# A softmax-attention and gated-MLP kernel: sign words of the weights by GpSimd, shift and sign in one VectorE instruction, weight pieces in pairs, the second k load with its channels reordered

## The chip, the cores and the metric

The kernel runs on one core of a Trainium2 chip. The metric is the device time of one execution in microseconds (us), the median of three runs. Five engines take part: TensorE (PE in the profile, its weight loads PEld), VectorE (DVE), ScalarE (ACT), GpSimd (POOL) and SyncE (SP), which only issues DMAs here.

## The reference

Attention without a score matrix: softmax of q over the head's channels, softmax of k over the sequence, their product with v, and on the result a gated MLP in which a learned matrix mixes positions.

```
q_s = softmax(q, axis=-1); k_s = softmax(k, axis=2)          # q, k, v: (8, 8, 576, 64)
kv  = einsum('bhsd,bhse->bhde', k_s, v)
x   = einsum('bhsd,bhde->bhse', q_s, kv)  -> (8, 576, 512)
h   = gelu_tanh(x @ w_in)                                    # w_in: (512, 1024)
u, v = h[..., :512], h[..., 512:]
v_n = (v - mean(v)) / sqrt(var(v) + 1e-6) * g_ln
v_s = einsum('ts,bsd->btd', w_sg, v_n) + b_sg                # w_sg: (576, 576)
out = x + (u * v_s) @ w_out                                  # w_out: (512, 512)
```

w_in, w_out and w_sg of the gated MLP come to the kernel as inputs; w_in and w_out are float64 in its memory, everything else float32.

## The kernel before

**Precision.** A product of two float32 matrices is made of three matmuls in the type fp32r: each operand is split into a high part (a cast) and a low part (the difference), and high x high, high x low and low x high are summed in PSUM. So each operand costs, beside the matmuls, one cast (mostly ACT) and one subtraction (DVE or POOL).

**Steps and order.** The work of the eight batches is cut into named steps such as `hu_mm 3 1`. The string PLAN (lines 33 to 137) writes all of them in one order. The class InOrder (line 144) makes every engine issue its instructions in exactly that order, so PLAN fixes five queues at once, SP's DMAs among them; an instruction that waits holds up everything behind it on its engine. A letter after a step (V, A or G) puts it on VectorE, ScalarE or GpSimd. All instructions but the matmuls (line 241) are recorded at line 154.

**Steps for one batch.** load_q, load_k, load_kt and load_v bring the operands. q is shifted by its maximum (q_max, q_swapm, q_top, q_sub), exponentiated, summed, scaled (q_inv, q_mul) and transposed (q_turn). For k, kt_max takes the maximum of each channel from the transposed load; kt_put and kt_get send the maxima through memory so that every partition holds all of them (kmt); k_sub (line 403) subtracts them and k_exp takes the exponential. kv_mm and x_mm are the attention products; x_high and x_low split x. hv_mm makes the v half of the MLP (hv_stat, hv_pow, hv_norm, hv_high, hv_low are the LayerNorm and its split: vnh, vnl), hu_mm the u half (hu_gelu), sg_mm the mixing of positions, gate the product with u, gate_high and gate_low its split (gh, ulow), out_mm the last product, out_add and out_rest the sum with x, out_store the store. The last block of the last batch is done in two halves: last_mm, last_add, last_store.

**The start.** Batch 0 has its own steps (q0_..., k0_..., x0_..., hu0_mm), which transpose on TensorE with an identity matrix (eye) that is loaded (load_eye). The weights arrive meanwhile, as float64: two 32-bit words to a number, the top one with sign and exponent. converter (line 274) makes a float32 of them in five steps for each piece of 128 columns (w_in: wi_..., eight pieces; w_out: wo_..., four pieces): a: ACT scales the top word, taken as a float, by 2^-112; b: DVE shifts the result left by three; c: DVE takes the sign bit of the top word with an AND and joins it with an OR; d: DVE shifts the low word right by 29 and joins it; h: ACT casts to the high part; l: POOL, DVE, or TensorE and ACT (wi_x and `wi_l A`) make the low part. c and d are scalar_tensor_tensor instructions, with two tensors as inputs (STT below), b is a tensor_scalar with one. The raw words lie in tiles that are later reused (raw_vnl holds pieces 2 and 3 of w_in, raw_vnh 0 and 1, raw_wo_h and raw_wo_l 4 to 7; raw_x_h and raw_x_l those of w_out); the words under work lie in four slots of the output (ot_i, ot_o). w_sg is split by ws_h and ws_l, 640 columns at a time. hu0_mm needs pieces 0 to 3, hv_mm needs 4 to 7.

## Time and profile before

| what | value |
|---|---|
| median of 3 runs | 504.43 us (503.58 to 504.43) |
| profiled execution | 504.85 us, its span 503.1 us |
| granted TensorE clock | 1.00 |
| instructions | 9377 |
| DMA | 57.28 MB, mean 114 GB/s |

How to read it: the span is the part of the execution that the profile covers; the time on top of it, 1.75 us here, is outside every engine's records. Busy time of an engine is a sum over its instructions; neighbouring instructions overlap a little, so the step from one start to the next can be shorter than a duration. A row of groups gives line, engine, operation, tiles, shape and count, then busy time and the mean in ns of one, then the idle time of the engine just before them with its releaser.

### The profile page before, as it was taken

To read this page: it belongs to the slowest core of one execution; us is meant where nothing else is said; L and a number is where in the kernel's file an instruction comes from. 1 tells how busy PE (TensorE), PEld (TensorE's weight loads), DVE (VectorE), ACT (ScalarE), POOL (GpSimd) and SP (SyncE) were. 2 spreads that over 40 slices of the span, in tenths; PEclk is the share of its full clock that TensorE was granted. 3 is DMA by queue.
4 is the path that set the end of the run, shared out by engine and by line. 5 is a ranking of instruction groups with operands and counts; after the bars stand their busy time and mean duration, and the time that the engine had idled before them with its cause. 6 is when DMAs were issued, how large, how long until landed. Compare 5 with 4: busy or idle time off the path is not lost.

```text
span 503.1 us, 9377 instructions
## 1 busy us (share of the span) xinstructions
PE 484.9 (96%) x3834; PEld 444.4 (88%) x3834; DVE 347.9 (69%) x563; ACT 246.9 (49%) x434; POOL 171.6 (34%) x180
## 2 busy tenths in 40 slices
...
GB/s 309 327 407 225 151 196 26 77 171 137 145 42 71 170 172 128 33 191 124 122 72 71 182 140 26 143 26 213 163 1 1 61 36 1 1 48 1 25 7 112
DMA packets 20495, 57.28 MB, mean 114 GB/s; under 512 B 3042, under 2 KB 3428, under 8 KB 20452
## 3 DMA queue, kind: packets, MB, share of 16 engines
...
q14 instruction: 13, 0.11, 0.1%
...
## 4 chain that ended last, share of the span: by engine, by line
PE 82%; DVE 5%; DMA 4%; ACT 3%; issue 3%; POOL 2%; SPq 1%; POOLq 0%; DVEq 0%; ACTq 0%
PE ps L241 82%; DVE qq L154 2%; DMA kk<-kt 1%; DMA kmt<-scr 1%; DMA eye<-identity 1%; POOL kk L154 1%; SPq L154 1%; POOL qe L154 1%; POOL ulow L154 1%; DVE kk L154 0%; DVE ulow L154 0%; DVE u L154 0%; DVE ot_i L154 0%; DVE wo_l L154 0%; ACT qs L154 0%
## 5 line engine op out<-in xcount | busy, mean ns | idle before, releaser
L154 POOL TENSOR_TENSOR rs<-ve,half 128x1 f32<-128x1 f32 x36 | 27.4, 765 | 111.8 <-DVE ve L154 101.8
L241 PE MATMUL ps<-ulow,wo_h 128*128 128x288 f32 x256 | 55.7, 296 | 1.2 <-DVE ulow L154 1.2
L241 PE MATMUL ps<-gh,wo_h 128*128 128x288 f32 x256 | 56.0, 298 | 0.5 <-DVE o L154 0.5
L241 PE MATMUL ps<-ws_h,vnl 128*128 128x288 f32 x256 | 54.9, 296 | 1.0 <-DVE vnl L154 1.0
L241 PE MATMUL ps<-gh,wo_l 128*128 128x288 f32 x256 | 55.5, 295 | 0.0
L241 PE MATMUL ps<-ws_h,vnh 128*128 128x288 f32 x256 | 55.2, 297 | 0.1
L154 DVE TENSOR_TENSOR u<-ps,u 128x576 f32<-128x576 f32 x32 | 23.9, 753 | 44.9 <-PE ps L241 44.7
L241 PE MATMUL ps<-ws_l,vnh 128*128 128x288 f32 x256 | 54.9, 296 | 0.0
L154 ACT CAST gh<-u 128x576 fp32r<-128x576 f32 x32 | 21.4, 672 | 64.9 <-DVE u L154 64.9
L154 ACT ACTIVATE u<-ps 128x576 f32<-128x576 f32 (+2 forms) x36 | 21.4, 603 | 53.9 <-PE ps L241 53.8
L241 PEld LDWEIGHTS ps<-ws_h,vnh 128*128 128x128 f32 x256 | 41.7, 188 | 1.9 <-ACT u L154 1.2
L241 PEld LDWEIGHTS ps<-gh,wo_h 128*128 128x128 f32 x256 | 41.7, 188 | 1.9 <-DVE o L154 0.8
L241 PE MATMUL ps<-x_h,wi_h 128*128 128x288 f32 (+2 forms) x256 | 42.4, 300 | 0.9 <-ACT u L154 0.9
L154 ACT ACT_TABLE_LOAD x30 | 38.5, 1283 | 9.3 <-PE ps L241 5.3
L241 PEld LDWEIGHTS ps<-ulow,wo_h 128*128 128x128 f32 x256 | 41.2, 188 | 1.7 <-DVE ulow L154 1.7
L241 PEld LDWEIGHTS ps<-ws_h,vnl 128*128 128x128 f32 x256 | 41.3, 188 | 1.2 <-DVE vnl L154 1.2
L154 POOL TENSOR_TENSOR ulow<-u,gh 128x576 fp32r<-128x576 f32 x12 | 17.3, 1439 | 73.5 <-DVE ulow L154 50.2
L241 PEld LDWEIGHTS ps<-x_h,wi_h 128*128 128x128 f32 x256 | 36.5, 188 | 5.8 <-ACT u L154 2.8
L241 PE MATMUL ps<-x_l,wi_h 128*128 128x288 f32 (+2 forms) x256 | 41.5, 297 | 0.1
L241 PEld LDWEIGHTS ps<-gh,wo_l 128*128 128x128 f32 x256 | 41.4, 188 | 0.0
L241 PEld LDWEIGHTS ps<-ws_l,vnh 128*128 128x128 f32 x256 | 41.3, 188 | 0.0
L241 PE MATMUL ps<-x_h,wi_l 128*128 128x288 f32 (+2 forms) x256 | 41.3, 296 | 0.0
...
## 6 DMA issues: line engine op xcount, KB each, us to landing
...
```

Source lines behind the costliest of these rows:

```text
L154: ins = op(*args, **kw)
L241: tc.keep_in_program_order(nc.tensor.matmul(*args, **kw))
```

## The change

Five things change.

1. **The sign.** A new step b on GpSimd multiplies the top words, taken as floats, by 0.0 in place; what is left of each is its sign. Step c on VectorE then shifts t and joins the sign in one STT, so a piece takes two VectorE instructions instead of three. Step a may go to GpSimd (`wi_a 2 G`, 1, 0, and `wo_a` 2, 0).
2. **Pairs.** Pieces 4+5 and 6+7 of w_in and 0+1 and 2+3 of w_out (PAIRED) are handled together in instructions of 1024 columns. The words under work lie in one tile (o) that is the output tile later. w_sg is split two pieces at a time, 1280 columns.
3. **k.** For batches 2 to 7 the transposed load has its rows in another order, so that the 256 maxima that k_sub reads lie side by side; before, it read every fourth word.
4. **The end.** `last_mm 7 0, last_mm 7 1` stand ahead of `last_add 7 0`; before, `last_add 7 0` stood between them.
5. **The order.** PLAN is written anew, for all engines. load_eye is the seventh DMA instead of the tenth. Of the twelve k_subs, GpSimd had eight and VectorE four; now GpSimd has four and VectorE eight.

The diff of the functions that the prediction speaks of (PLAN left out but for lines that show steps of the weights):

```
-q0_turn 0 0, q0_inv 0 1, k0_max 0 3, k0_copy 0 2, q0_mul 1 0, q0_sum 1 1, q0_inv 1 1, q0_turn 1 0, k0_less 0 3, k0_max 0 0, wi_a 2, wi_b 2
+k0_less 1 1, wi_l 6 V, hu0_mm 2 0 1, hu0_mm 2 1 1, hu0_mm 3 0 0, hu0_mm 1 1 1, wi_h 4, wi_l 4 V, hu0_mm 1 1 0, q_sum 1 0, q_sum 1 1, wo_a 2 G
...
+PAIRED = (("i", 4), ("i", 6), ("o", 0), ("o", 2))
...
-        def scale(f):
+        def scale(f, E=A):
 
             top, low, t = word(kind, f)
-            A.activation(f32(t), f32(top), AF.Copy, scale=2.0 ** -112)
-
-        def shift(f):
-            t = word(kind, f)[2]
-            V.tensor_scalar(out=t, in0=t, scalar1=3, scalar2=None, op0=ALU.logical_shift_left)
+            if E is A:
+                A.activation(f32(t), f32(top), AF.Copy, scale=2.0 ** -112)
+            else:
+                E.tensor_scalar(out=f32(t), in0=f32(top), scalar1=2.0 ** -112, scalar2=None, op0=ALU.mult)
 
         def sign(f):
             top, low, t = word(kind, f)
-            V.scalar_tensor_tensor(out=t, in0=top, scalar=0x80000000, in1=t, op0=ALU.bitwise_and, op1=ALU.bitwise_or)
+            G.tensor_scalar(out=f32(top), in0=f32(top), scalar1=0.0, scalar2=None, op0=ALU.mult)
+
+        def shift(f):
+            top, low, t = word(kind, f)
+            V.scalar_tensor_tensor(out=t, in0=t, scalar=3, in1=top, op0=ALU.logical_shift_left, op1=ALU.bitwise_or)
...
-        return scale, shift, sign, rest, high, low_
+        return scale, sign, shift, rest, high, low_
...
     def k_sub(b, h, E=V):
         kk = kk_s(b, h, at=h)
         k4 = kk.rearrange("p t (a c) -> p t a c", a=2)
-        top = tops(b)[1].rearrange("p (c n) -> p n c", n=NP)[:, None, 2 * h:2 * h + 2]
+        top = tops(b)[1].rearrange("p (n c) -> p n c", n=NP)[:, None, 2 * h:2 * h + 2]
         E.tensor_tensor(out=k4, in0=k4, in1=top.broadcast_to(k4.shape), op=ALU.subtract)
...
-    arr["kt"] = np.ascontiguousarray(k.transpose(0, 1, 3, 2)).reshape(B, NP, P, S)
+    rows = np.ascontiguousarray(k.transpose(0, 1, 3, 2))
+    turned = rows.reshape(B, P, NP, S).transpose(0, 2, 1, 3)
+    arr["kt"] = np.concatenate([rows[:2].reshape(2, NP, P, S), turned[2:]])
```

What the new order does to the queues is shown at three places; the numbers behind tile names tell buffers apart. VectorE's queue at the start, from the maximum of the last k load of batch 0 on, before:

```order
L154 TENSOR_REDUCE k0m<-ukt_130 128x1
L154 TENSOR_SCALAR ot_i_175<-ot_i_175 128x512
L154 TENSOR_TENSOR qq_1_102<-qq_1_102,qd_1_141 128x640
L154 SCALAR_TENSOR_TENSOR ot_i_175<-raw_vnl,ot_i_175 128x512
L154 TENSOR_TENSOR qq_0_95<-qq_0_95,qd_0_110 128x640
L154 SCALAR_TENSOR_TENSOR ot_i_175<-raw_vnl,ot_i_175 128x512
L154 TENSOR_SCALAR kr_1_231<-ps_0_80 128x2
L154 RECIPROCAL kr_1_231<-kr_1_231 128x2
L154 TENSOR_SCALAR ot_i_227<-ot_i_227 128x512
L154 TENSOR_SCALAR ot_i_217<-ot_i_217 128x512
```

and in the changed kernel from the same maximum on:

```order
L154 TENSOR_REDUCE k0m<-ukt_171 128x1
L154 SCALAR_TENSOR_TENSOR o<-o,raw_vnl 128x512
L154 SCALAR_TENSOR_TENSOR o<-raw_vnl,o 128x512
L154 TENSOR_SCALAR qd_0_109<-qd_0_109 128x10
L154 RECIPROCAL qd_0_109<-qd_0_109 128x10
L154 TENSOR_TENSOR qq_0_96<-qq_0_96,qd_0_109 128x640
L154 TENSOR_SCALAR kr_1_221<-ps_0_81 128x2
L154 RECIPROCAL kr_1_221<-kr_1_221 128x2
L154 SCALAR_TENSOR_TENSOR o<-o,raw_vnl 128x512
L154 TENSOR_TENSOR kvt_1_243<-ps_0_81,kr_1_221 128x128
L154 SCALAR_TENSOR_TENSOR o<-raw_vnl,o 128x512
```

The shifts (TENSOR_SCALAR on ot_i) are gone, each piece has two STT, the first of which reads o and the signed top word, and one product of batch 0's q stands between them.

GpSimd's queue at the start, before, from its last two q products to the first maxima of batch 1:

```order
L154 TENSOR_TENSOR qq_0_95<-qq_0_95,qd_0_110 128x512
L154 TENSOR_TENSOR qq_1_102<-qq_1_102,qd_1_141 128x512
L154 TENSOR_TENSOR ws_66<-vb_93,ws_66 1x320
L154 TENSOR_TENSOR ws_66<-vb_94,ws_66 1x320
L154 TENSOR_TENSOR wi_l<-ot_i_227,wi_h 128x4x128
L154 TENSOR_TENSOR wi_l<-ot_i_235,wi_h 128x4x128
L154 COPY qs_1_341<-qm_1_314 32x36 x4
```

and in the changed kernel over the same stretch:

```order
L154 TENSOR_TENSOR qq_1_98<-qq_1_98,qd_1_126 128x640
L154 TENSOR_SCALAR raw_vnl<-raw_vnl 128x512
L154 TENSOR_SCALAR o<-raw_vnl 128x512
L154 TENSOR_SCALAR raw_vnl<-raw_vnl 128x512
L154 TENSOR_SCALAR o<-raw_vnh 128x512
L154 TENSOR_SCALAR raw_vnh<-raw_vnh 128x512
L154 TENSOR_SCALAR o<-raw_vnh 128x512
L154 TENSOR_SCALAR raw_vnh<-raw_vnh 128x512
L154 TENSOR_TENSOR ws_66<-vb_94,ws_66 1x320
L154 TENSOR_TENSOR ws_66<-vb_95,ws_66 1x320
L154 TENSOR_TENSOR wi_l<-o,wi_h 128x4x128
L154 COPY qs_0_312<-qm_0_310 32x36 x4
```

Seven one-input instructions on the raw words (four signs on raw_vnl and raw_vnh in place, three scales into o) now stand ahead of the two bias parts (ws_66), and one low part instead of two is left behind them.

VectorE's queue in the middle, where the gated values of batch 0 are split, before:

```order
L154 TENSOR_TENSOR ulow_0_1013<-u_0_779,gh_0_1011 128x576
L154 TENSOR_SCALAR ve_1_1018<-sv_1_876 128x1
L154 TENSOR_TENSOR u_3_518<-ps_1_78,u_3_518 128x576
L154 TENSOR_TENSOR qm_1_958<-qm_1_958,qs_1_960 128x36
L154 TENSOR_TENSOR u_2_545<-ps_0_77,u_2_545 128x576
L154 TENSOR_TENSOR wo_l<-ot_o_594,wo_h 128x4x128
L154 TENSOR_TENSOR u_1_505<-ps_2_79,u_1_505 128x576
L154 TENSOR_REDUCE ktall_1089<-kmt_0_956 128x1
L154 TENSOR_TENSOR qq_1_954<-qq_1_954,qm_1_958 128x1152
L154 TENSOR_TENSOR ulow_1_1110<-u_1_505,gh_1_1108 128x576
L154 TENSOR_TENSOR ulow_2_1112<-u_2_545,gh_2_1085 128x576
```

and in the changed kernel:

```order
L154 TENSOR_TENSOR u_1_471<-ps_2_80,u_1_471 128x576
L154 SCALAR_TENSOR_TENSOR vn_72<-v_4_758,rs_4_802,vn_72 64x512
L154 TENSOR_TENSOR ulow_1_1032<-u_1_471,gh_0_890 128x576
L154 TENSOR_SCALAR ve_1_1034<-sv_1_975 128x1
L154 TENSOR_TENSOR ulow_2_1038<-u_2_469,gh_1_967 128x576
L154 TENSOR_TENSOR ulow_3_1040<-u_3_449,gh_1_967 128x576
L154 TENSOR_REDUCE ktall_1042<-kmt_0_979 128x1
L154 TENSOR_REDUCE qd_1_1060<-qq_1_841 128x36
L154 TENSOR_TENSOR kk_1_684<-kk_1_684,kmt_4_989 128x1280
L154 TENSOR_TENSOR kk_0_682<-kk_0_682,kmt_4_989 128x1280
L154 TENSOR_SCALAR ve_2_1072<-sv_2_1064 128x1
```

The two subtractions of batch 2's k maxima (kk, kmt) now stand in VectorE's queue behind the four splits; before, they stood in GpSimd's queue.

276 lines of the change are left out of this document (141 added, 135 removed).

## The prediction

> **What bounds the kernel now.** The page comes first: who is busy, and what the chain that ends last is made of.
>
> ```profile
> PE 484.9 (96%) x3834; PEld 444.4 (88%) x3834; DVE 347.9 (69%) x563; ACT 246.9 (49%) x434; POOL 171.6 (34%) x180
> PE 82%; DVE 5%; DMA 4%; ACT 3%; issue 3%; POOL 2%; SPq 1%; POOLq 0%; DVEq 0%; ACTq 0%
> ```
>
> TensorE (PE) is the bound: 484.9 of 503.1 us. The change takes no matmul out of the long stages, so it can only win what PE idles, 18.2 us, or lose by making PE idle more. The waits of PE come next, to see where the 18.2 lie (total, times, longest).
>
> ```profile
> PE ps L241 <- DMA eye<-identity: 9.6, 1, 9.6
> PE ps L241 <- DVE ulow L154: 1.2, 2, 1.0
> PE ps L241 <- DVE vnl L154: 1.0, 1, 1.0
> PE ps L241 <- ACT u L154: 0.9, 1, 0.9
> PE ps L241 <- POOL qq L154: 0.6, 1, 0.6
> PE ps L241 <- DVE o L154: 0.5, 1, 0.5
> PE ps L241 <- DVE vn L154: 0.4, 1, 0.4
> ```
>
> More than half is the wait for the first data, and the rest is a few single waits behind DVE and POOL. The table of windows puts them in time (columns: length, then busy of PE, PEld, DVE, ACT and POOL with counts, clock, DMA).
>
> ```profile
> 36.00:70.00 34.00, 34.00 (x261) 28.00 (x261) 32.47 (x65) 29.31 (x69) 13.96 (x16) 1.00 0.52 189
> 90.00:98.00 8.00, 6.77 (x43) 5.96 (x42) 7.96 (x9) 7.75 (x10) 1.94 (x1) 1.00 0.35 120
> 150.00:160.00 10.00, 9.42 (x132) 9.08 (x131) 6.91 (x8) 5.43 (x8) 8.49 (x9) 1.00 0.22 61
> 190.00:200.00 10.00, 8.46 (x57) 7.58 (x56) 9.70 (x13) 7.77 (x11) 4.78 (x7) 1.00 0.29 102
> 400.00:408.00 8.00, 7.05 (x60) 6.20 (x59) 4.60 (x10) 3.24 (x6) 0.00 (x0) 1.00 0.21 77
> ```
>
> From 36 to 70 us PE never idles although DVE is 32.47 us busy: work taken off DVE there is worth nothing by itself. PE loses 1.23, 0.58 and 1.54 us in the three windows at 90, 150 and 190, and 0.95 at 400. So three places can move the time: the start (whatever comes before PE runs without a gap), those windows, and the tail.
>
> **The start.** Three rows of PE's timeline date it: the first matmul, the first u block of batch 0 (hu0_mm), the first LayerNorm product (hv_mm 0).
>
> ```profile
> 9.62 2.37 PE L241 MATMUL ps<-eye,ukt 128*128 128x128 f32 x10 [9.62 <-DMA eye<-identity]
> 27.44 0.39 PE L241 MATMUL ps<-x_h,wi_h 128*128 128x256 f32 x2
> 37.58 1.09 PE L241 MATMUL ps<-wi_h,x_h 128*128 128x512 f32 x4
> ```
>
> The earlier identity load brings nothing: the first matmul of the new order transposes exp(k) of its second load. ACT's exp of the second k load runs 9.33 to 10.11 before, and nothing in the change makes that transfer much faster.
>
> ```profile
> 9.33 0.78 ACT L154 ACTIVATE ukt<-ukt,k0m 128x576 f32<-128x576 f32 x1 [0.22 <-DVE k0m L154]
> ```
>
> Then the weights. The durations of the converter's steps and of POOL's nearest rows:
>
> ```profile
> L154 DVE TENSOR_SCALAR ot_i<-ot_i 128x512 uint32<-128x512 uint32 x8 | 3.3, 423 | 0.0
> L154 DVE SCALAR_TENSOR_TENSOR ot_i<-raw_vnl,ot_i 128x512 uint32<-128x512 uint32 x4 | 2.7, 686 | 0.0
> L154 POOL TENSOR_TENSOR qq<-qq,qm 128x512 f32<-128x512 f32 x2 | 2.1, 1044 | 3.9 <-DVE qm L154 3.9
> L154 POOL TENSOR_TENSOR wi_l<-ot_i,wi_h 128x512 fp32r<-128x512 f32 x5 | 6.5, 1322 | 16.2 <-ACT wi_h L154 16.2
> L154 POOL COPY qs<-qm 32x36 f32<-32x36 f32 x32 | 8.6, 270 | 18.1 <-DVE qm L154 16.7
> ```
>
> DVE instructions overlap at their ends: this shift started at 14.14 and the next instruction at 14.48, a step of 0.34, and a STT (scalar_tensor_tensor) steps by 0.60 (28.46 to 29.06).
>
> ```profile
> 14.14 0.43 DVE L154 TENSOR_SCALAR ot_i<-ot_i 128x512 uint32<-128x512 uint32 x1
> 14.48 0.82 DVE L154 TENSOR_TENSOR qq<-qq,qd 128x640 f32<-128x640 f32 x1
> 28.46 0.68 DVE L154 SCALAR_TENSOR_TENSOR ot_i<-raw_wo_h,ot_i 128x512 uint32<-128x512 uint32 x1
> 29.06 0.69 DVE L154 SCALAR_TENSOR_TENSOR ot_i<-raw_wo_l,ot_i 128x512 uint32<-128x512 uint32 x1
> ```
>
> Twelve shifts go: 12 x 0.34 = 4.1 us less DVE, four of them (1.4 us) before hu0_mm can run. I walked the new DVE order at these steps. From the last k maximum on, some 8.8 us of instructions stand ahead of the last rest step of piece 1, from 11.6 us, so it starts at 20.3. If nothing holds DVE up, hu0_mm starts near 24.6 with short waits in it and hv_mm 0 near 36.6: 1.0 us before 37.58.
>
> A wait is added: each combined STT waits for POOL's sign of its piece, and behind it on DVE stand the last q product of batch 0 and the kv scale, for which PE's x products wait. On POOL the same time now holds seven 128x512 one-input instructions (four signs, three scales) ahead of its bias parts and wi_l 1. Their price x is in no row. COPY of 36 columns (0.27) is a floor, the broadcast two-input form (1.04) a ceiling; POOL falls from 1.32 to 1.04 when one of two full inputs becomes a broadcast, so a further 0.28 down, 0.77, is one estimate, and half of 1.32, 0.66, one that counts the input streams. I take 0.65, at the lower of the two.
>
> What this does to DVE depends on whether the two engines exclude each other. For instructions with two inputs they do:
>
> ```profile
> 84.36 7.58 POOL L154 TENSOR_TENSOR kk<-kk,kmt 128x1280 f32<-128x1280 f32 x2
> 89.73 3.43 DVE L154 TENSOR_TENSOR qq<-qq,qm 128x1152 f32<-128x1152 f32 x1
> 184.90 2.51 DVE L154 TENSOR_TENSOR kk<-kk,kmt 128x1280 f32<-128x1280 f32 x1 [2.92 <-DMA kmt<-scr]
> 186.66 4.21 POOL L154 TENSOR_TENSOR kk<-kk,kmt 128x1280 f32<-128x1280 f32 x1 [4.37 <-DMA kk<-k]
> 187.33 4.75 DVE L154 TENSOR_TENSOR qq<-qq,qm 128x1152 f32<-128x1152 f32 x1
> 26.86 1.35 DVE L154 TENSOR_TENSOR qq<-qq,qm 128x1152 f32<-128x1152 f32 x1
> 150.30 3.16 POOL L154 COPY qe<-qd 32x36 f32<-32x36 f32 x4
> ```
>
> The same DVE instruction takes 1.35 us alone, 3.43 and 4.75 beside POOL's k_sub: each time it ends about 1.2 us after POOL's has ended (91.94 and 190.87). The last row shows a one-input POOL form held up too (3.16 for four copies, while a DVE k_sub ran to 152.63). No row shows a one-input POOL instruction long enough to hold up DVE. I take it that it does. [...]
>
> With strict turns each of the seven pieces pushes DVE's STT chain by x, less about 0.6 us that PE fills with the x products of batch 0 meanwhile: start = -1.0 - 0.6 + 7x. At 0.65 that is **+2.9 us**; at 0.27 it is +0.3, at 1.04 +5.7; without any hold-up -1.0. ACT, which gives three scales to POOL (3 x 0.6), is not last in that chain, so its relief is taken at nothing.
>
> **From 40 to 70 us** the remaining DVE steps run 1024 wide in pairs, and POOL signs them. PE ran through this stage on 261 matmuls without a gap and does so at a price of nothing as long as the normalised values are ready for the first gate matmul; the cover is DVE's spare time, 34.00 - 32.47 = 1.5 us, plus 8 x 0.34 = 2.7 us of shifts gone. If six wide POOL signs and scales of 2x = 1.3 us each (7.8 us) all held DVE up, 3.6 us would come on top; POOL is only 13.96 busy there, so most of them find DVE in instructions that read PSUM or one input, and I take 0.
>
> **The middle.** k_sub is the subtraction of the column maximum; its second operand was read with a step of four words and now lies side by side.
>
> ```profile
> L154 DVE TENSOR_TENSOR kk<-kk,kmt 128x1280 f32<-128x1280 f32 x4 | 11.7, 2921 | 6.1 <-DMA kmt<-scr 6.1
> L154 POOL TENSOR_TENSOR kk<-kk,kmt 128x1280 f32<-128x1280 f32 x8 | 32.0, 4006 | 11.2 <-DMA kmt<-scr 6.8 <-DMA kk<-k 4.4
> ```
>
> On DVE it takes 2.51 us undisturbed, 1.96 ns an element, where qq<-qq,qm takes 1.35/1152 = 1.17: at that rate 1.5 us. On POOL 4.0 should fall to between 1280 x 1.32/512 = 3.3 and 1280 x 1.04/512 = 2.6. [...] The new order also gives POOL four k_subs instead of eight: 32.0 us become about 4 x 3 = 12. DVE's eight now cost 8 x 1.5 = 12, as its four did.
>
> The windows at 90 and 190 lie behind k_subs of POOL for batches 2 and 4, through DVE's qq and then ulow, vnl and vn, for which PE waits. In the new order both batches have theirs on DVE, so those 2.77 us lose their cause; of the 0.58 at 150 (batch 3, one of two still on POOL) half. Middle: **-3.0 us**. Bounds: -4.3 with the window at 400 as well, and +1.0 if the new order makes as many waits elsewhere and one more of the longest kind (1.0). What is late next is the eight k_subs in DVE's queue, with hv_low and gate_low behind them; 1.5 us there is within DVE's 31% of free time.
>
> **The tail.**
>
> ```profile
> 497.28 0.29 PE L241 MATMUL ps<-gh,wo_l 128*128 128x288 f32 x1
> 497.61 0.46 DVE L154 TENSOR_TENSOR o<-ps,o 128x288 f32<-128x288 f32 x1 [0.83 <-PE ps L241]
> 498.12 0.40 PE L241 MATMUL ps<-gh,wo_h 128*128 128x288 f32 x1 [0.55 <-DVE o L154]
> 500.01 0.46 DVE L154 TENSOR_TENSOR o<-ps,o 128x288 f32<-128x288 f32 x1 [1.94 <-PE ps L241]
> ```
>
> PE's second half waited for the addition of the first. In the new order its 12 matmuls follow at their own step of 0.13 us: 498.12 - 497.41 = 0.7 sooner. But now both additions come behind the last matmul, one after the other, which gives back 0.4. Tail: **-0.3** (0 to -0.7).
>
> **Sum.** 2.9 - 3.0 - 0.3 = -0.4. The profiled execution took 504.85 us (span 503.1 and 1.75 outside it), 0.42 above the median of the three runs, 504.43; the steps are differences, so I set them against the median: **504.0 us**.
>
> **The rivals.**
> A, slower: POOL's one-input pieces are as dear as its broadcast form. The place is DVE's STT chain before hu0_mm; x = 1.04 gives +5.7 - 3.0 - 0.3 = +2.4, 506.8, and with the wide pieces' 3.6 us uncovered up to 510. It decides from x = 0.85 (7 x 0.85 - 1.6 - 3.3 = +1.0). For it: POOL has no row of this width under 1.04. Against: those rows read two operands.
> B, faster: POOL's one-input pieces don't hold DVE up, or mostly meet DVE's one-input and PSUM instructions, of which as many stand between. Then -1.0 - 3.0 - 0.3 = -4.3, 500.1; with half of the turns taken, so half-way between -1.0 and 2.9, 502.1. For it: in 22 to 84 us nearly every DVE row has its undisturbed length.
> C, the reordering doesn't do what it says: k_sub keeps 2.5 and 4.0, eight of them load DVE with 20 us instead of 12, and the windows stay. Then 2.9 + 0 - 0.3 = +2.6, 507.0. Against it: the two rates above.
>
> **How the numbers follow.** About 0.2%, 1.0 us, is what a measurement of this kernel can tell from no change. Forecast 0.36: 502.8 to 505.5 for x between about 0.5 and 0.85; of it 0.11 is faster by over 1.0 us, 0.20 within, 0.05 slower. A 0.28, slower. B 0.29, faster. C 0.07, of it 0.05 slower, 0.02 within. Faster 0.40, same 0.22, slower 0.38. Cases of both signs hold most of the chance, so the range has to reach into A and B: 499.8 to 507.8; the forecast's own is 502.8 to 505.5.
>
> **What would show it.** Start: the step from hu0_mm's first matmul to hv_mm 0's, and hv_mm 0's own start (40.5 by the forecast, 36.6 by B, over 42 by A); DVE STT rows on raw_vnl and raw_vnh well above 0.69 us show the hold-up, and POOL's TENSOR_SCALAR row shows x. Middle: k_sub near 1.5 on DVE and 3 on POOL, PE's waits for vnl, vn and ulow gone. Tail: no wait of PE for o, and two additions of 0.46 in a row at the end. The prediction is wrong if x is under 0.4 or over 0.9, if STT rows stay at 0.69 beside POOL's pieces, or if PE has new waits between 70 and 490 us that sum to over 2 us.

## The result and the profile after

The changed kernel takes 511.83 us, the median of four runs (510.25 to 514.03), against 504.43 (503.58 to 504.91): 1.0152 times the time before (95% interval 1.0112 to 1.0192). The forecast was 504.0 within 499.8 to 507.8, so the result lies 4 us above the range, and above rival A's 506.8 and its upper end, 510, too. The profiled execution took 511.75 us, its span 509.9.

The page of the changed kernel, busy times and the chain that ended last:

```profile
PE 484.7 (95%) x3834; PEld 445.2 (87%) x3834; DVE 339.3 (67%) x546; ACT 250.6 (49%) x429; POOL 172.6 (34%) x180
PE 76%; DVE 7%; ACT 7%; DMA 5%; issue 2%; POOL 1%; SPq 1%; DVEq 0%; POOLq 0%; ACTq 0%
```

PE still has 3834 matmuls and is busy as long as before (484.9), so the longer span is idle PE. DVE became 8.6 us shorter, as intended, and POOL hardly busier in sum: the signs and scales take 29.9 us of it at the start, while k_sub fell from 32.0 to 11.8 and the low parts of w_in from 6.5 to 1.3. The waits of PE say where it idles:

```profile
PE ps L241 <- ACT ukt L154: 10.2, 1, 10.2
PE ps L241 <- ACT u L154: 7.0, 3, 5.5
PE ps L241 <- ACT x_h L154: 2.3, 1, 2.3
PE ps L241 <- DVE u L154: 1.2, 1, 1.2
PE ps L241 <- DVE ve L154: 0.3, 1, 0.3
```

The waits of before for ulow, vnl, vn and qq are gone, and two are new and large: 5.5 us for u and 2.3 for x_h. Windows put them in time (length; busy PE, PEld, DVE, ACT, POOL with counts; clock; DMA):

```profile
20.00:28.00 8.00, 5.58 (x75) 3.40 (x77) 6.40 (x10) 5.41 (x14) 7.67 (x7) 1.00 0.74 252
36.00:46.00 10.00, 4.55 (x30) 4.29 (x29) 9.97 (x10) 6.89 (x11) 4.60 (x2) 0.79 0.90 354
46.00:49.00 3.00, 3.00 (x11) 2.46 (x10) 2.40 (x6) 0.00 (x0) 2.54 (x10) 0.55 0.06 22
90.00:98.00 8.00, 8.00 (x54) 7.52 (x53) 7.39 (x11) 7.85 (x14) 2.52 (x2) 1.00 0.29 76
190.00:200.00 10.00, 10.00 (x60) 8.91 (x59) 7.18 (x11) 4.79 (x7) 3.65 (x7) 1.00 0.21 59
```

The windows at 90 and 190, in which PE idled before, are full. All of the loss is ahead of 49 us: POOL is busy in 7.67 of 8.00 us from 20 to 28, where PE works 5.58; from 36 to 46 PE works 4.55 of 10 us; and from 46 to 49 it is busy throughout, but at a granted clock of 0.55.

**A clean cut between start and middle.** The first gate matmul of batch 0 (sg_mm 0 0) follows on the same 490 matmuls in both orders (a record more or less apart). Its row before, and then in the changed kernel:

```profile
70.73 0.43 PE L241 MATMUL ps<-ws_h,vnh 128*128 128x288 f32 x2
```

```profile
80.53 0.43 PE L241 MATMUL ps<-ws_h,vnh 128*128 128x288 f32 x2
```

So the start lost 9.8 us, and from there to the end of the span 503.1 - 70.7 = 432.4 became 509.9 - 80.5 = 429.4, a gain of 3.0. The forecast had +2.9 for the start and -3.3 for the rest. The sum was wrong in one term, the first. One window up to that matmul, for both kernels:

```profile
0.00:70.73 70.73, 60.45 (x490) 48.74 (x491) 65.89 (x129) 58.32 (x118) 28.50 (x35) 1.00 0.73 271
```

```profile
0.00:80.53 80.53, 62.48 (x491) 50.19 (x491) 70.34 (x111) 56.54 (x100) 51.78 (x44) 0.96 0.65 239
```

Idle PE went from 10.3 to 18.1 us (+7.8), and the matmuls themselves take 2.0 more, with the clock at 0.96. POOL went from 28.5 to 51.8 us of work, on 44 instructions instead of 35. DVE has 18 instructions fewer and yet 4.5 us more busy time.

**What PE waits for.** PE's rows at the start, first transpose, first u block, the long wait and the first LayerNorm product:

```profile
10.19 2.40 PE L241 MATMUL ps<-eye,ukt 128*128 128x128 f32 x10 [10.19 <-ACT ukt L154]
...
28.75 0.50 PE L241 MATMUL ps<-x_h,wi_h 128*128 128x256 f32 x2
...
45.05 0.79 PE L241 MATMUL ps<-x_h,wi_h 128*128 128x256 f32 x2 [5.45 <-ACT u L154]
...
46.49 1.91 PE L241 MATMUL ps<-wi_h,x_h 128*128 128x512 f32 x4
```

Against before they are late by 0.57, 1.31 and, at hv_mm 0, 46.49 - 37.58 = 8.9 us. The stretch from hu0_mm to hv_mm 0 grew from 10.1 to 17.7, and holds the whole of the 5.45. It names ACT; here is ACT's timeline over that wait:

```profile
38.52 1.05 ACT L154 CAST wi_h<-o 128x1024 fp32r<-128x1024 f32 x1 [2.02 <-DVE o L154]
39.48 0.77 ACT L154 ACTIVATE kk<-kk,k0m 128x576 f32<-128x576 f32 x1
40.92 1.05 ACT L154 CAST wi_h<-o 128x1024 fp32r<-128x1024 f32 x1 [0.67 <-DVE o L154]
41.87 0.77 ACT L154 ACTIVATE kk<-kk,k0m 128x576 f32<-128x576 f32 x1
42.66 1.28 ACT L154 ACT_TABLE_LOAD   x1
43.95 1.65 ACT L154 ACTIVATE u<-ps 128x320 f32<-128x320 f32 x5
```

The matmul that waits is `hu0_mm 2 0 0`. It writes the first half of a PSUM tile whose second half `hu0_gelu 2 1` has yet to read; the wait is for the whole tile, and it goes when the block stands ahead of that read (e5 below, where the longest wait for it is 1.2 us). In ACT's queue that gelu stands behind the casts of both wide pairs, two exponentials and a table load, and each cast waits for DVE's o: for the pieces that POOL signs. So a step of the u block that needs none of the pieces 4 to 7 waits for all of them.

**What POOL takes.** Groups of the changed kernel up to 60 us:

```profile
L154 POOL TENSOR_SCALAR raw_vnh<-raw_vnh 128x512 f32<-128x512 f32 x2 | 3.6, 1792 | 0.2
L154 POOL TENSOR_SCALAR raw_vnl<-raw_vnl 128x512 f32<-128x512 f32 x2 | 3.3, 1674 | 1.3 <-ACT o L154 1.2
L154 POOL TENSOR_SCALAR o<-raw_vnh 128x512 f32<-128x512 f32 x2 | 3.2, 1588 | 0.0
L154 POOL TENSOR_SCALAR raw_wo_h<-raw_wo_h 128x1024 f32<-128x1024 f32 x1 | 2.9, 2942 | 0.0
L154 POOL TENSOR_SCALAR raw_wo_l<-raw_wo_l 128x1024 f32<-128x1024 f32 x1 | 2.9, 2932 | 0.1
L154 POOL TENSOR_SCALAR o<-raw_vnl 128x512 f32<-128x512 f32 x1 | 1.5, 1533 | 0.0
```

The seven pieces of 512 columns take 3.6 + 3.3 + 3.2 + 1.5 = 11.6 us, 1.66 each; the forecast's price was 0.65, and its ceiling 1.04. The six wide signs and scales of 1024 columns take 2.8 to 2.9 each, but for one of 3.7. VectorE's rows beside them:

```profile
22.21 1.12 DVE L154 SCALAR_TENSOR_TENSOR o<-o,raw_vnh 128x512 uint32<-128x512 uint32 x1 [1.50 <-POOL raw_vnh L154]
23.37 0.69 DVE L154 SCALAR_TENSOR_TENSOR o<-raw_vnh,o 128x512 uint32<-128x512 uint32 x1
...
31.76 2.16 DVE L154 TENSOR_TENSOR qq<-qq,qm 128x1152 f32<-128x1152 f32 x1
34.55 2.14 DVE L154 SCALAR_TENSOR_TENSOR o<-o,raw_wo_l 128x1024 uint32<-128x1024 uint32 x1 [0.63 <-DMA raw_x_l<-w_out]
```

DVE waits 1.50 for a sign, and through ACT's queue that makes PE's wait of 2.3 for x_h: the cast of x_h stands there behind the cast of a weight piece, which itself waited 2.11 for DVE's last step on that piece. DVE is also held up, but only in part: the q product at 31.76 takes 2.16 instead of 1.35 and ends at 33.92, while POOL's sign of the pair, started at 31.59, runs to 34.52.

### The profile page after: what moved, and what is told of

The parts are those of the page before. It is cut to its first block, busy times and chain, and to the rows that moved or that the text cites. A ratio compares the mean times of both kernels' runs of the same rounds, so it can differ in the third digit from the quotient of the medians.

```text
span 509.9 us, 9340 instructions
## 1 busy us (share of the span) xinstructions
PE 484.7 (95%) x3834; PEld 445.2 (87%) x3834; DVE 339.3 (67%) x546; ACT 250.6 (49%) x429; POOL 172.6 (34%) x180
## 3 DMA queue, kind: packets, MB, share of 16 engines
q1 hardware_dynamic: 20452, 56.68, 33.2%
## 4 chain that ended last, share of the span: by engine, by line
PE 76%; DVE 7%; ACT 7%; DMA 5%; issue 2%; POOL 1%; SPq 1%; DVEq 0%; POOLq 0%; ACTq 0%
PE ps L241 76%; ACT L154 2%; DMA raw_wo_h<-w_in 2%; DMA kk<-k 1%; DVE v L154 1%; DVE o L154 1%; DMA raw_x_h<-w_out 1%; SPq L154 1%; DMA qq<-q 1%; DVE vnl L154 1%; ACT kk L154 1%; ACT v L154 1%; ACT u L154 1%; DVE qd L154 1%; DVE kk L154 1%
## 5 line engine op out<-in xcount | busy, mean ns | idle before, releaser
L154 POOL TENSOR_TENSOR rs<-ve,half 128x1 f32<-128x1 f32 x36 | 24.4, 683 | 97.6 <-DVE ve L154 94.1
L154 ACT ACTIVATE vnh<-v,rs 128x512 fp32r<-128x512 f32 x32 | 22.5, 723 | 37.2 <-POOL rs L154 22.6
L241 PE MATMUL ps<-wi_h,x_h 128*128 128x512 f32 x144 | 40.7, 405 | 0.0
```

The source lines that it names most:

```text
L154: ins = op(*args, **kw)
L241: tc.keep_in_program_order(nc.tensor.matmul(*args, **kw))
```

## The experiments

Theories. P: POOL's one-input steps are dear, and the weights' chain waits for them. Q: the rewritten order makes PE wait for the half-read PSUM tile whatever POOL costs. L: the weights' loads come later in the new SP queue. C: the low clock. And for the gain after the gate, K: it comes from k_sub's operand; or N: from the new order. The expectations, written ahead of each run, call P theory 1, L theory 2 and Q (later the new order as a whole) theory 3.

| run | against before (95%) | hv_mm 0, us | first gate matmul, us | from it to the end |
|---|---|---|---|---|
| before | 1 | 37.58 | 70.73 | 432.4 |
| after | 1.0152 (1.0112 to 1.0192) | 46.49 | 80.53 | 429.4 |
| e1_sign_on_vector | 1.0198 (1.0137 to 1.0258) | 45.71 | 85.93 | 429.6 |
| e2_no_weights_on_gpsimd | 1.0247 (1.0193 to 1.0300) | 46.77 | 88.47 | 429.0 |
| e3_loads_first | 1.0178 (1.0158 to 1.0197) | 48.88 | 82.81 | 429.8 |
| e4_before_sign_on_gpsimd | 1.0174 (1.0152 to 1.0196) | 43.64 | 80.00 | 432.3 |
| e5_u_block_ahead_of_gelu | 1.0197 (1.0175 to 1.0219) | 43.86 | 85.38 | 429.5 |
| e6_matmuls_in_the_wait | 1.0111 (1.0087 to 1.0136) | 47.62 | 80.62 | 428.0 |
| e7_in_weights_as_before | 1.0158 (1.0125 to 1.0192) | 40.95 | 82.59 | 429.7 |
| e8_before_k_and_tail | 0.9901 (0.9882 to 0.9920) | 37.85 | 70.99 | 426.9 |
| e9_cheap_gpsimd_steps | 1.0111 (1.0071 to 1.0151) | 42.74 | 77.14 | 429.0 |
| e11_e8_with_warm_start | 0.9912 (0.9888 to 0.9937) | 37.78 | 70.93 | 427.0 |
| e12_after_with_old_k_load | 1.0195 (1.0156 to 1.0234) | 48.52 | 82.33 | 430.8 |
| e13_cheap_and_u_block_ahead | 0.9973 (0.9946 to 0.9999) | 37.93 | 70.91 | 429.3 |
| e14_before_cheap_sign | 1.0017 (0.9999 to 1.0036) | 37.83 | 71.07 | 433.3 |
| e15_sign_by_two_input_form | 1.0283 (1.0247 to 1.0319) | 45.48 | 88.43 | 428.0 |
| e16_u_block_ahead_late_split | 1.0153 (1.0124 to 1.0183) | 42.43 | 78.94 | 428.5 |
| e17_in_weights_as_before_late_split | 1.0087 (1.0057 to 1.0117) | 40.92 | 77.70 | 431.7 |
| e18_no_gpsimd_weights_late_split | 1.0076 (1.0047 to 1.0105) | 40.31 | 76.59 | 430.5 |

They are told by question; the numbers give the order in which they ran. The first LayerNorm product (hv_mm 0) and the gate cut the start in two places; one profiled execution stands behind each of these times. The probe e10 (1.0097) is told below. What follows on the gate stays between 428.0 and 431.7 in the new order, so what the edits of the start do is in the two columns ahead of it.

The totals of e1, e2, e3, e4, e5, e7 and e15 came out above every range that had been written down for them, by 0.5 to 5.8 us. e8 came out 2.0 us better than expected.

**How far one trace can be trusted.** In the old order the two times repeat: before, e8, e10 and e11 share the start (e11 adds 14 matmuls to it) and lie within 0.3 us of each other. In the new order they don't. Up to hv_mm 0, e12 is the program of after, and e16 that of e5, and yet they differ by 2.0 and 1.4 us. In after and e16, POOL's first wide sign starts just ahead of DVE's second q product (31.59 against 31.76). In e12, e5, e3 and e6 the product starts first (32.41 in e12), the sign starts at 32.7 to 33.0 and takes longer (3.54 us in e12 instead of 2.93), and DVE's next STT waits longer for it, in e12:

```profile
36.59 2.13 DVE L154 SCALAR_TENSOR_TENSOR o<-o,raw_wo_l 128x1024 uint32<-128x1024 uint32 x1 [2.83 <-POOL raw_wo_l L154]
```

So two traces of the new order are best compared when the same engine came first in both: after with e16, and e12 with e3, e5 and e6.

### The sign in the old order: is POOL's price enough by itself?

e4: the kernel before, with nothing but the sign moved to POOL and the two DVE instructions made one, in its own old order.

```diff
-            V.tensor_scalar(out=t, in0=t, scalar1=3, scalar2=None, op0=ALU.logical_shift_left)
-            V.scalar_tensor_tensor(out=t, in0=top, scalar=0x80000000, in1=t, op0=ALU.bitwise_and, op1=ALU.bitwise_or)
+            G.tensor_scalar(out=f32(top), in0=f32(top), scalar1=0.0, scalar2=None, op0=ALU.mult)
+            V.scalar_tensor_tensor(out=t, in0=t, scalar=3, in1=top, op0=ALU.logical_shift_left, op1=ALU.bitwise_or)
```

> The kernel before with only the converter changed: step b is the sign on GpSimd (twelve of 128x512), step c joins shift and sign in one STT; PLAN, pieces and k as before. Theory 1: twelve instructions of 1.6 us, 19 us more on GpSimd before 60 us, with its low parts behind them; 507 to 512. Theory 2 and 3 (the new order is what costs): VectorE has 12 x 0.34 us less, GpSimd was free there, 503.5 to 505.5.

Ratio 1.0174: the start loses 9.3 us with none of the new order in it. The window up to the gate, and POOL's first sign group:

```profile
0.00:80.00 80.00, 64.57 (x490) 50.98 (x491) 68.39 (x118) 59.56 (x118) 50.48 (x47) 0.96 0.65 241
```

```profile
L154 POOL TENSOR_SCALAR raw_vnl<-raw_vnl 128x512 f32<-128x512 f32 x2 | 3.8, 1908 | 1.8 <-ACT ot_i L154 1.8
```

e14 is e4 with the sign on a quarter of the columns, the same twelve instructions in the same places; it leaves out the signs of the other three quarters.

```diff
-            G.tensor_scalar(out=f32(top), in0=f32(top), scalar1=0.0, ...)
+            some = top[:, 0:top.shape[1] // 4]
+            G.tensor_scalar(out=f32(some), in0=f32(some), scalar1=0.0, ...)
```

> Run e4 (the order before, signs on GpSimd, shift and sign joined on VectorE) with the sign over a quarter of the columns; signs of the other three quarters are left out. If the 1.5 us that each sign takes is what cost 9 us in e4, the first gate matmul comes back from 80.0 to between 70 and 73 us and the total to 503.5 to 506.5, as the kernel before or a little better. If it is the wait for another engine in the middle of VectorE's chain, it stays at 76 to 80 and 509 to 513.

```profile
0.00:71.07 71.07, 60.32 (x491) 48.78 (x492) 65.02 (x117) 58.42 (x118) 39.10 (x47) 1.00 0.73 270
```

The gate is back at 71.07, the ratio at 1.0017. The same instructions, waits and semaphores with less length cost nothing: in the old order the loss is POOL's time, P alone. In e4 VectorE's waits for signs sum to 5.8 us up to 45 us. The twelve shifts that VectorE is rid of in e14 win nothing either: hv_mm 0 comes at 37.83, and before had it at 37.58.

### Price and wait in the new order

Three kernels with the changed one make a square. e9 makes the signs a quarter as wide and the GpSimd scales a memset (it leaves out the signs of three quarters of the columns and the values of those scales):

```diff
-                E.tensor_scalar(out=f32(t), in0=f32(top), scalar1=2.0 ** -112, ...)
+                E.memset(f32(t), 0.0)
```

> The changed kernel with GpSimd's share of the converter made cheap: each sign instruction runs over a quarter of its columns, and each scale on GpSimd is a memset of its tile. Signs of three quarters of the columns and those scales are left out; order, waits and all other instructions stay. Theory 1 (the price of GpSimd's one-input instructions delays the start): the first gate matmul, which follows the same 490 matmuls in every version, comes at 70 to 74 us instead of 80.5, total 500.5 to 505. Theory 3 (the new order itself, above all the later casts of pieces 4 to 7 and VectorE's longer way to the x product of batch 1): it stays at 77 to 82, total 507.5 to 512.

e5 puts the waiting u block ahead of the gelu, so that it no longer has to wait for that read of the tile:

```diff
-hu0_mm 2 1 0, hu0_gelu 2 1, hu0_gelu 1 1, ... wo_b 2, hu0_mm 2 0 0, q_inv 1 0
+hu0_mm 2 1 0, hu0_mm 2 0 0, hu0_gelu 2 1, hu0_gelu 1 1, ... wo_b 2, q_inv 1 0
```

> The changed kernel with one step of PLAN moved: hu0_mm 2 0 0 stands ahead of hu0_gelu 2 1 instead of five steps behind it. No engine's order changes; only the wait goes that this block of matmuls has for a gelu which reads the other half of the same PSUM tile. Theory 3 (the new order made PE wait for ScalarE's gelu, which stands behind the casts of pieces 4 to 7): PE's wait for ACT u of 5.5 us becomes one for wi_h of about 2 us (the last cast ends at 41.97), the later matmuls move up by 3 to 4 us, and with less low clock 506.5 to 509.5. Theory 1 (the weights themselves are late, because of GpSimd): the same wait is only renamed and stays over 4 us; 510 to 512.

e13 is both edits together.

> Run e9 (cheap steps on GpSimd; signs of three quarters of the columns and the scales on GpSimd left out) together with the one moved step of e5, hu0_mm 2 0 0 ahead of hu0_gelu 2 1. If the price of the GpSimd steps and the wait on the half-read PSUM tile are what delays the start, PE goes on at 38.8 us with the first product of the v half instead of 41.8, and the first gate matmul comes at 72.5 to 74.5 us, total 503 to 506.5. If it is VectorE's longer way in the new order, PE waits for the transposes of batch 1 instead, the gate matmul stays at 76 to 78 and the total at 507.5 to 511.

| hv_mm 0, us | u block behind the gelu | u block ahead of it |
|---|---|---|
| POOL at full price, sign first | 46.49 (after) | 42.43 (e16) |
| POOL at full price, product first | 48.52 (e12) | 43.86 (e5) |
| POOL cheap | 42.74 (e9) | 37.93 (e13) |

(e16, told below, differs from e5 only behind hv_mm 0.) At hv_mm 0 the cheap steps alone give 3.8 us, the moved u block alone 4.1 (4.7 in the second row), and both together 8.6, which brings hv_mm 0 and the gate (70.91) back to where before had them. So P and Q are both true, and neither is enough by itself: e9's gate, 77.14, and its total lie in the range that was expected if the order costs, not in that of the price. With the price gone, the wait for the half-read tile is still there, as PE's row of e9 shows:

```profile
41.78 0.51 PE L241 MATMUL ps<-x_h,wi_h 128*128 128x256 f32 x2 [3.39 <-ACT u L154]
```

But e5, 4.7 us ahead of e12 at hv_mm 0, is 3.1 behind it at the gate (2.6 ahead of after and 4.9 behind it). What it lost in between is the subject of the next two parts.

### Giving the work back, or taking a cheaper form

e1 takes the sign back to DVE in the new order; e2 takes the scales back to ACT too; e7 is e5 with the w_in pieces converted as before and the w_out pieces by POOL.

```diff
         def sign(f):
-            G.tensor_scalar(out=f32(top), in0=f32(top), scalar1=0.0, ...)
+            pass
         def shift(f):
-            V.scalar_tensor_tensor(out=t, in0=t, scalar=3, in1=top, ...)
+            V.tensor_scalar(out=t, in0=t, scalar1=3, scalar2=None, op0=ALU.logical_shift_left)
+            V.scalar_tensor_tensor(out=t, in0=top, scalar=0x80000000, in1=t, op0=ALU.bitwise_and, op1=ALU.bitwise_or)
```

> The changed kernel with the signs back on VectorE: step b does nothing, step c is again a shift (tensor_scalar) and a STT with AND and OR, and PLAN is as in the changed kernel. GpSimd keeps the scales of pieces 0 to 2 and of w_out. Theory 1 (the price of GpSimd's one-input instructions, 1.6 us for 512 and 2.9 us for 1024 columns, makes GpSimd the queue that everything at the start waits for): GpSimd loses 4 x 1.7 + 4 x 2.9 = 18 us there, PE's wait of 5.5 us for the gelu shrinks below 2 us and the low clock behind it goes; 504.5 to 507.5. Theory 2 (the weights of pieces 4 to 7 land late, because their loads stand behind a q load that waits for its buffer): nothing changes, 510 to 513. Theory 3 (the order on ScalarE, where the gelus stand behind the casts of pieces 4 to 7): the wait shrinks only as far as those casts come earlier, 507 to 511.

e2 adds to that:

```diff
-            if E is A:
-                A.activation(f32(t), f32(top), AF.Copy, scale=2.0 ** -112)
-            else:
-                E.tensor_scalar(out=f32(t), in0=f32(top), scalar1=2.0 ** -112, ...)
+            A.activation(f32(t), f32(top), AF.Copy, scale=2.0 ** -112)
```

> The changed kernel with signs on VectorE as before the change (shift and STT) and all scales on ScalarE, PLAN unchanged: GpSimd has none of the one-input instructions. Theory 1: all of their 27 us on GpSimd goes, 503.5 to 506.5, unless ScalarE, which gets 5 scales of 0.6 to 1.2 us, becomes the queue. Theory 2: 510 to 513. Theory 3: ScalarE is later still, 508 to 513.

e7 makes both edits under a condition, on the order of e5:

```diff
-            if E is A:
+            if E is A or kind == "i":
```

> Run e5 with the converter of w_in as before the change (scales on ScalarE; shift and sign on VectorE), while w_out keeps its scales and signs on GpSimd. GpSimd has no instruction on the raw words before 41 us. Theory 1: pieces 4 to 7 are cast by 39.5 instead of 42 us, PE's wait behind 39 us is under 1 us, 504 to 507. Theory 3 (what the new order does to VectorE and ScalarE): VectorE gets 4 x 0.34 + 2 x 0.6 us of shifts back on its chain and the first x products wait longer, 507 to 512.

None of the three is faster than the changed kernel. In e1 and e2 the wait for u is still there (3.6 and 6.4 us): ACT's gelus start at 43.6 and 44.2 us, where after has them at 43.95, because the second cast waits 1.3 and 1.4 us for VectorE, which has the shifts back, and in e2 a scale of w_out stands ahead of the gelus too. So in this order the gelus, and with them hv_mm 0 (45.71 and 46.77), come as late with POOL free of the signs. e7, without that wait, has hv_mm 0 at 40.95, 5.5 us ahead of after, and yet the gate at 82.59.

e15 is e5 with the two-input form that a row of before priced at 1.04:

```diff
-            G.tensor_scalar(out=f32(top), in0=f32(top), scalar1=0.0, ...)
+            G.tensor_tensor(out=f32(top), in0=f32(top), in1=zero.broadcast_to(top.shape), op=ALU.mult)
```

> Run e5 with GpSimd's signs and scales as tensor_tensor, times a broadcast column (0.0, 2^-112), instead of tensor_scalar: the same result. The broadcast two-input form took 1.04 us for 512 columns in the kernel before, tensor_scalar 1.5. If the price decides, GpSimd gets 7 x 0.5 + 6 x 0.9 = 9 us back, the first gate matmul comes 1.5 to 4 us earlier than the 85.4 of e5, total 510 to 513 where e5 had 514.4. If two inputs exclude VectorE for the whole instruction, as k_sub does, VectorE loses that again: 514 to 518.

It is the slowest run, 1.0283, just above what was expected if two inputs exclude DVE. The groups show a cheaper POOL and a dearer DVE:

```profile
L154 POOL TENSOR_TENSOR raw_vnl<-raw_vnl,zero 128x512 f32<-128x512 f32 x2 | 2.4, 1214 | 1.3 <-ACT o L154 1.3
...
L154 DVE SCALAR_TENSOR_TENSOR o<-raw_vnl,o 128x512 uint32<-128x512 uint32 x2 | 2.7, 1372 | 0.0
L154 DVE SCALAR_TENSOR_TENSOR o<-o,raw_wo_l 128x1024 uint32<-128x1024 uint32 x1 | 2.9, 2944 | 1.8 <-POOL raw_wo_l L154 1.8
```

The STTs, 0.68 in the changed kernel, take 1.37, and the wide one 2.94, where it takes 1.2 alone: what POOL saves, DVE pays, and PE waits 7.0 for DVE's kvt ahead of its x products of batch 1.

### The second place: GpSimd's split of w_sg

From hv_mm 0 to the gate before takes 33.2 us and after 34.0, but e1, e2, e5 and e7 take 40 to 42. In all four the same thing stands there. Three rows of e5's timeline, one each of POOL, DVE and PE:

```profile
60.42 3.97 POOL L154 TENSOR_TENSOR ws_l<-ghws,ws_h 128x1280 fp32r<-128x1280 f32 x1
...
61.58 3.89 DVE L154 SCALAR_TENSOR_TENSOR o<-raw_x_h,o 128x1024 uint32<-128x1024 uint32 x1
...
68.74 2.96 PE L241 MATMUL ps<-qt,kvt 64*64 64x288 f32 x16 [2.66 <-DVE qt L154]
```

POOL's low part of the first pair of w_sg, two full inputs over 1280 columns, covers a wide STT, which takes 3.89 us instead of 1.2 and ends 1.1 after POOL's has. Batch 1's transposed q (qt) stands behind it on DVE, PE waits 2.66 for that, and its next products run slowly (2.96 for what takes 1.20 otherwise; clock 0.68 from 70 to 78). In the changed kernel the same POOL instruction starts at 62.78, 0.1 us behind the last wide STT; there it is POOL's that takes longer (3.98, where it takes 2.99 alone in e16), and the STT has its 1.22. Theory S: it is this meeting that undid the gain. Theory O: the new order as such relies on the shorter DVE queue. Three kernels move that one instruction behind a later step of the LayerNorm: e16 is e5 so, e17 is e7, and e18 is e2 with the u block ahead of the gelu.

```diff
-ws_h 0, ws_l 0, kv_mm 1 1, ... hv_pow 0 3, hv_high 0 3
+ws_h 0, kv_mm 1 1, ... hv_pow 0 3, ws_l 0, hv_high 0 3
```

> The changed kernel with the u block ahead of the gelu (as in e5), and the low part of the mixing weights' first pair (GpSimd, two full inputs, 4.0 us) placed behind the third row of the LayerNorm's reciprocal root instead of ahead of batch 1's second kv product. Theory S (second place): in e5 the u block's move did win 2.6 us at the first LayerNorm product (43.86 against 46.49), and then lost 7.5 on the way to the gate, because this 4.0 us GpSimd instruction met a 1024-wide VectorE one (3.89 instead of 1.23 us), behind which PE waited 2.66 for qt and then ran at a low clock. Then here: first LayerNorm product near 43.9, no VectorE STT over 2.3 us between 55 and 70, no wait for qt, gate near 79 (77.5 to 80.5), ratio 1.006 to 1.012. Rival theory O (the order itself, whatever meets whatever): gate stays near 85, ratio near 1.02.

> e7 (w_in pieces converted by ScalarE and VectorE as before, w_out pieces by GpSimd, u block ahead of the gelu) with the same low part placed later. Theory S: first LayerNorm product stays near 41, no wait for qt, gate near 76 (74.5 to 78), ratio 1.001 to 1.008. Rival theory O: gate stays near 82.6, ratio near 1.016.

> e2 (no sign and no scale on GpSimd at all) with the u block ahead of the gelu and the same low part placed later. Theory S: the wait of 6.4 us for u is gone, the first LayerNorm product comes near 41 (40 to 43), no wait for qt, gate near 75 (73.5 to 78), ratio 1.000 to 1.008; then the new order without GpSimd's weights is no worse than the old one but for the rest of the start. Rival theory O (the new order relies on the shorter VectorE queue): PE waits for VectorE elsewhere by as much, gate 82 or later, ratio over 1.014.

The wait for qt is gone in all three, and the gate comes at 78.94, 77.70 and 76.59. From hv_mm 0 to the gate takes 36.5, 36.8 and 36.3 us, 5.0, 4.9 and 5.4 less than in e5, e7 and e2, and some 3 more than before. So the meeting is worth about 5 us in the traces; S holds there and O falls. In the ratio e17 (1.0087) and e18 (1.0076) are faster than e7 and e2, and e18 clearly faster than the changed kernel, at the upper end of what was expected or just over it. e16's (1.0153) missed its 1.006 to 1.012, and its interval touches that of e5 (1.0197): the profile of e5 is of the slowest of its four runs (516.73, median 514.42), that of e16 of the fastest (509.20, median 511.91), so their traces show more between them than their medians, 2.5 us. And e18, with nothing of the weights on POOL and both order faults mended, is still 5.9 us late at the gate. It starts 1.0 later and has waits of 0.6 to 1.5 us spread over the start; which rows of the new order make these wasn't tried.

### The price by itself

e10 is e8 (below) with a row of POOL instructions on a free tile in the last batch, some with a DVE addition beside them: a multiplication of 512 columns side by side, of every other word in place, from every other word to side by side, of 1024 columns, and a copy.

```diff
+    def probe():
+        times(a[:, 0:512])
+        times(every(a, 512))
+        times(every(a, 512), c[:, 0:512])
+        times(a[:, 0:1024])
...
+        G.tensor_copy(out=c[:, 0:512], in_=c[:, 512:1024])
```

> The kernel of run e8 with eight extra GpSimd instructions near 430 us on an idle tile, where GpSimd has nothing to do for 30 us, and two extra VectorE additions beside them. If the step of two words (the raw words lie eight bytes apart) makes the sign dear, the 512-column multiplication takes 0.7 to 0.9 us side by side and 1.5 with the step, and 1024 columns side by side 1.4 to 1.7. If it is the operation, 512 columns take 1.5 and 1024 take 2.9 side by side too. An addition on VectorE (0.75 us alone) beside a GpSimd instruction ends within 1 us of its start if GpSimd holds it up for only a part of its length, and after GpSimd's end if it excludes it. Total as in e8, 499 to 500.5.

POOL's instructions on that tile (lowest, median and highest duration in ns, then the stretch of starts in us):

```profile
L154 POOL TENSOR_SCALAR qqp<-qqp x6: 1497/1550/3337, 457.2 to 468.7; 128x512 f32<-128x512 f32 x4, 128x1024 f32<-128x1024 f32 x2
L154 POOL COPY qqp<-qqp x1: 609/609/609, 468.2 to 468.2; 128x512 f32<-128x512 f32 x1
```

The four multiplications of 512 columns, side by side or at every other word, took 1.50 to 1.56 us: the 8-byte step of the raw words costs at most 0.06. A copy of the same size takes 0.61. It is the operation that is dear, not the layout and not the neighbour on DVE. The run's total (1.0097) is no statement on the kernel, and the expected total was missed: the probe delayed the last LayerNorm, and PE waited 5.6 us for it.

### The loads

e3 issues the loads of pieces 6, 7, 4 and 5 ahead of `load_q 1 1`. In the changed kernel that q load waits in SP's queue for its buffer from 16.6 to 21 us, and those pieces land behind it, at 29.9 to 32.5 (24.4 to 29.6 before).

```diff
-kv_scale 0 1, q0_turn 0 1, load_q 1 1, x0_mm 1 0, ...
+kv_scale 0 1, q0_turn 0 1, load_w_in 6, load_w_in 7, load_w_in 4, load_w_in 5, load_q 1 1, x0_mm 1 0, ...
```

> The changed kernel with the loads of pieces 6, 7, 4, 5 put ahead of the two q loads of batch 1 in SyncE's queue, nothing else: they can be issued near 11 us instead of 21 to 24, and land near 20 to 24 instead of 28 to 32.5. Theory 2: the sign of pieces 6 and 7 can start 6 us earlier, the 5.5 us wait goes, 504 to 507. Theory 1: GpSimd is busy with pieces 0 to 3 until 25.5 and with the bias and a low part until 28.6, so only the start of the wide signs at 31.6 moves, by at most 3 us, and the total falls by 0 to 3: 508.5 to 512.

1.0178, no gain. The four pieces are issued from 12.5 to 13.8 us there and land by about 24, but POOL starts its first wide sign at 32.76, behind copies of q's maxima that come later (29.70, after 28.66); PE still waits 6.2 for u. So L is out as the cause.

### The clock

e6 puts 20 matmuls, whose result nobody reads, into the 5.45 us wait.

```diff
-wo_b 2, hu0_mm 2 0 0,
+wo_b 2, warm, hu0_mm 2 0 0,
```

> The changed kernel with 20 extra matmuls of 512 columns (4.7 us at full clock, their result is not used) put into PE's wait at 39.3 us. They take away no wait of any other engine. If the low granted clock from 45.05 to 48.4 us (the first product there stepped by 0.43 us instead of 0.23) follows from PE having stood still for 5.5 us, the clock stays at 1.00 behind the wait and the time falls by about 2 us, to 508.5 to 510.5. If the clock falls for another reason, the time is as before or up to 1 us longer, 511 to 513.

PE's rows of e6 there:

```profile
41.13 4.85 PE L241 MATMUL ps<-x_h,minus 128*128 128x512 f32 x20
...
46.80 0.50 PE L241 MATMUL ps<-x_h,wi_h 128*128 128x256 f32 x2 [0.83 <-ACT u L154]
47.62 1.08 PE L241 MATMUL ps<-wi_h,x_h 128*128 128x512 f32 x4
```

The first LayerNorm product takes 1.08 where it took 1.91, and from the u block to the gate it is 80.62 - 46.80 = 33.8 instead of 80.53 - 45.05 = 35.5. The granted clock from 36 to 70 us is 1.00 in e6 and 0.90 in after. So the slow clock behind the wait is worth 1.7 us. The u block itself came 1.75 later than in after, since in e6 DVE's product came first, so the gate didn't move against after; against e12, where it came first too, the gate is 1.7 earlier (82.33). The ratios of e6 and after overlap. C is real but second: a result of the wait.

e11 tries the same at the start of e8: 14 matmuls on 64 rows ahead of the first transposes.

```diff
-load_q0 0 0, q0_max 0 0, q0_sub
+load_q0 0 0, warm, q0_max 0 0, q0_sub
```

> The kernel of run e8 with 14 matmuls on a cleared tile ahead of the first transposes, from about 2 us on, while PE waits for its data. If standing still is what makes the first matmuls slow (ten transposes took 2.37 us at 9.62 and 1.25 at 46.09), they run at 0.11 us each and the batch-0 products come up to 1 us earlier; 498.3 to 499.3. If VectorE and ScalarE set the pace up to 27 us, the total stays as in e8, 499.5.

```profile
3.50 6.34 PE L241 MATMUL ps<-vn 64*128 64x512 f32 x14 [3.50 <-DVE vn L154]
9.77 2.39 PE L241 MATMUL ps<-eye,ukt 128*128 128x128 f32 x10
```

They ran for 6.34 us without a gap, 0.45 each where e6's took 0.24, and the ten transposes behind them still took 2.39, as without them (2.37 before; 1.25 for ten at 46.09). 0.9912 against 0.9901: nothing. The granted clock is 0.999 over the whole of e11, and 1.00 from 9.6 to 12 us in before, so what makes these rows slow is not shown, and stays open.

### The middle: operand or order?

e8: the kernel before with the k reordering and the tail, and nothing else of the change.

```diff
-        top = tops(b)[1].rearrange("p (c n) -> p n c", n=NP)[:, None, 2 * h:2 * h + 2]
+        top = tops(b)[1].rearrange("p (n c) -> p n c", n=NP)[:, None, 2 * h:2 * h + 2]
...
-last_add 7 0, last_mm 7 1, last_store 7 0
+last_mm 7 1, last_add 7 0, last_store 7 0
```

> The kernel before with two parts of the change alone: the transposed k load in the new order of channels (k_sub reads its maxima side by side), and last_mm 7 1 ahead of last_add 7 0. PLAN otherwise as before. If the step of four words is what made k_sub dear, it takes 1.5 us on VectorE and 2.9 on GpSimd, VectorE's qq behind it ends 1 us earlier each time, and PE's waits at 90 and 190 us (2.77 us) fall by half or more; with 0.3 at the tail 501.5 to 503.5 on a chip where the kernel before takes 504.4. If the step does not matter: k_sub as before, only the tail, 504.1.

499.47 us, 0.9901 (0.9882 to 0.9920): faster than both kernels, and the best version of the study. Its start is before's, and the gain after the gate is 432.4 - 426.9 = 5.5, of which 3.2 are idle PE (8.0 to 4.7). Its k_sub groups:

```profile
L154 DVE TENSOR_TENSOR kk<-kk,kmt 128x1280 f32<-128x1280 f32 x4 | 6.6, 1643 | 7.1 <-DMA kmt<-scr 7.1
L154 POOL TENSOR_TENSOR kk<-kk,kmt 128x1280 f32<-128x1280 f32 x8 | 26.1, 3270 | 12.1 <-DMA kmt<-scr 7.1 <-DMA kk<-k 5.0
```

2.92 became 1.64 on DVE and 4.01 became 3.27 on POOL, DVE's qq behind them went from 3.43 to 2.80 us, and PE's waits for vnl, vn and qq are gone although POOL still has eight k_subs. e12 is the other half: the changed kernel with the old k load and operand.

```diff
-        top = tops(b)[1].rearrange("p (n c) -> p n c", n=NP)[:, None, 2 * h:2 * h + 2]
+        top = tops(b)[1].rearrange("p (c n) -> p n c", n=NP)[:, None, 2 * h:2 * h + 2]
...
-    arr["kt"] = np.concatenate([rows[:2].reshape(2, NP, P, S), turned[2:]])
+    arr["kt"] = np.ascontiguousarray(k.transpose(0, 1, 3, 2)).reshape(B, NP, P, S)
```

> The changed kernel with the k load of before: k_sub reads every fourth word again, everything else stays. If the reordering is worth in the new order what it was in e8, k_sub takes 2.5 us on VectorE (eight of them, 8 us more in all) and 3.6 to 4 on GpSimd, new waits come up between 90 and 400 us, and the total rises by 2 to 6 us, to 514 to 518. If the gain of e8 came from the old order's waits only, it stays at 511 to 513. The first gate matmul stays at 80.5 by both.

1.0195, and 430.8 after the gate against 429.4: in the new order the operand is worth 1.4 us there, since the order had already taken the long POOL k_subs out of PE's way. (The ratios of e12 and after overlap; the 1.4 is from one trace each, and the gate itself came 1.8 later in e12, where the edit does nothing.) So K and N each remove most of the same waits, and K alone does more than both together: the new order costs some 429.4 - 426.9 = 2.5 us in the middle.

## Why the prediction was wrong, step by step

- **What bounds the kernel**: right. PE is the bound in every version (busy 96% of the span before, 95% after), and each version's time is PE's idle time plus what the clock costs it.
- **x = 0.65 us per one-input piece**: this is the first of two steps that failed, both in the term for the start. It measured 1.66 in the changed kernel and 1.50 to 1.56 alone (e10). The reasoning was that fewer inputs cost less, with the broadcast two-input form as ceiling (1.04). A copy (0.61) obeys that, but a multiplication by a scalar (1.50) is dearer than one by a broadcast column (1.04 before, 1.21 in e15). The bounds, from 36-column copies and two-input rows, held no row of the operation itself, so the upper one was no bound.
- **+2.9 us for the start**: measured +9.8. With x = 1.66 the formula -1.0 - 0.6 + 7x gives 10.0, but that is no proof of it. With the cheap steps of e9 (four signs at 0.55 and three memsets at 0.52, 3.8 in all) it would give +2.2, and hv_mm 0 came 5.2 late, 1.3 of it from a later first matmul, and the gate 6.4. That is the second step that failed: the formula lacks the wait for the half-read tile. So a right price alone would not have saved the forecast: e9's steps cost less than 0.65 a piece, and it still took 1.0111 times before, 510 us, above the range. Without that wait (e13) hv_mm 0 came only 0.35 late, 0.7 us of a later first matmul included, where the formula asks +2.2: its full turn for each piece is too much. That 1.66 gives almost the measured start is luck: two errors of opposite sign.
- **Strict turns of DVE and POOL**: wrong in detail. POOL's TENSOR_SCALAR holds a two-input DVE instruction up for 0.2 to 0.9 us, not for its whole length (2.16 against 1.35 at 31.76, with the sign running on for 0.6 after DVE's end). Where DVE starts first it is POOL that is held up, until DVE's end (3.54 in e12: the product ends at 33.77, 2.8 ahead of the sign's end). In the old order the signs cost mainly as inputs that DVE waits for (e4); in the changed kernel the hold-ups, some 3.5 us up to 40 us, are more than the 1.50 of waiting. That a one-input instruction of POOL holds DVE up for its whole length was the author's assumption, and no run shows it. The two-input forms come closer to it: beside them a wide STT took 3.89 in e5, where it ended 1.1 after POOL's had, and 2.94 in e15, both 1.2 alone.
- **Who waits behind an added wait**: half of it was missed. The prediction named the q product and the kv scale on DVE. It didn't name ACT's queue, where the gelu stands behind both wide casts, nor that the next u block writes the half-read tile. Both can be read from the order. Taking that wait away alone moves hv_mm 0 by 4.1 us (after and e16).
- **40 to 70 us at nothing**: right for the changed kernel, 34.0 us from hv_mm 0 to the gate against 33.2, the difference being mostly the slow clock behind the wait. But it was right by luck, by 0.1 us, the distance of POOL's start from the last wide STT: in four of its variants POOL's split of w_sg met a wide STT, and the stage cost 6 to 8 us more, some 5 of it by that meeting. The 3.6 that the prediction named for a lost cover was the right kind of price and too small, and it looked for it in the signs.
- **First matmul**: predicted unchanged, 0.57 later.
- **Middle -3.0**: measured -3.0 with the tail, -2.6 without it. But the reason was only partly right. The groups of the changed kernel:

```profile
L154 DVE TENSOR_TENSOR kk<-kk,kmt 128x1280 f32<-128x1280 f32 x8 | 13.3, 1667 | 7.3 <-DMA kmt<-scr 7.3
L154 POOL TENSOR_TENSOR kk<-kk,kmt 128x1280 f32<-128x1280 f32 x4 | 11.8, 2942 | 19.5 <-DMA kk<-k 15.9 <-DMA kmt<-scr 3.6
```

k_sub takes 1.48 us undisturbed on DVE (forecast 1.5; the mean of 1.67 holds one of 2.94) and 2.94 on POOL (forecast 3), and the windows at 90 and 190 lost their idle time. What the forecast gave to moving k_subs between engines, the operand does by itself (e8), and the new order has waits of its own for u and ve, 1.5 + 1.2 + 0.3 = 3.0 us past the gate; the prediction had put the mark for an error at 2. Of the 3.0 gained, idle PE shows 0.8 (8.0 to 7.1), and 2.2 are shorter busy time of the same matmuls; how the modelled ends share that out is open.
- **Tail -0.3**: measured -0.4 (from the first matmul of last_mm 7 0 to the end of the span, 7.3 us before and 6.9 now), as forecast by its rows, both additions in one piece at the end, behind the last matmul:

```profile
506.38 0.82 DVE L154 TENSOR_TENSOR o<-ps,o 128x288 f32<-128x288 f32 x2 [2.35 <-PE ps L241]
```

- **The rivals**: A named the right place and sign, and a price that was too low. B's condition, undisturbed DVE rows, nearly held at 22 to 84 us before the change and said nothing about a new operation. C, that the reordering doesn't work, is refuted by both kernels' k_sub rows.
